# Gate logits from fp32 products of four column groups in place of products of high and low parts

## The chip, the cores and the metric

The kernel runs on one core of one Trainium2 chip. The metric is the device time of one execution in microseconds, as the median of several runs.

## The reference, cut to what matters

Three stages follow each other: a block-sparse attention, a dense first network, and a mixture of eight experts of which each token visits one, up to a capacity.

```python
def reference(**kwargs):
    ...
    x = np.ascontiguousarray(attn_out.transpose(0, 2, 1, 3)).reshape(B * S, H * D)   # 1088 tokens, 512 wide
    x = _moe_ref(x=x, **moe_kwargs)
    return _moe2_ref(x=x, **moe2_kwargs)

def _moe_ref(x, w1, w2, w3, w_out):
    h = np.maximum(np.maximum(x @ w1, x @ w2), x @ w3)      # 768 wide
    return (h @ w_out).astype(np.float32)                   # x2, 512 wide

def _moe2_ref(x, w_gate, w1, w2, capacity):
    logits = x @ w_gate                                     # 512 x 8
    expert_idx = np.argmax(logits, axis=1)
    ...                                                     # softmax weight of the chosen expert,
    for i in range(N):                                      # tokens to their expert, up to capacity
        ...
    h = np.maximum(np.einsum('ecd,edf->ecf', disp, w1), 0.0)
    y = np.einsum('ecf,efd->ecd', h, w2)
    ...
    for i in range(N):
        if keep[i]:
            out[i] = gate_w[i] * y[expert_idx[i], pos[i]]
    return out.astype(np.float32)
```

The change touches `logits = x @ w_gate`, one number per token and expert. An expert is chosen by argmax, so the logits have to keep nearly full fp32 accuracy.

## The kernel before

**Stages.** Up to about 118 us the attention runs on TensorE (PE), and between its parts, from 29 us on, the first layer of the dense network (`h`, L426); behind the first layer come its second layer, `x2` (L708), and the experts. Most products are made of three products of a faster type (fp32r): each fp32 number is split in a high part, rounded to fp32r, and a low part, the rest; high by high, high by low and low by high are summed in PSUM. ScalarE (ACT) usually makes the high part by a copy with a cast, VectorE (DVE) or GpSimd (POOL) the low part by a subtraction. Splits that the next stage waits for are those of `w_out` (`wo_h`, `wo_l`; the chain of L309 to L328 runs over ACT, DVE and POOL) and of the experts' weights (`w1h`, `w1l`, `w2h`, `w2l`; L828 and L829).

**The second layer.** `moe_second` walks over four windows of tokens: 256, 288, 256 and 288 columns (windows 0 to 3). In each it makes x2, transposed, in four blocks d of 128 of the 512 features; a block is 18 matmuls (L708) into one PSUM bank. ACT copies a finished block to `x2T[:, d]` in fp32 (L714), DVE makes its high and low part (`x2h`, `x2l`, both named `x2hl`, L715 and L716), and two matmuls (L699, called a pair here) add the block's share to the logits `pl`, one PSUM bank of 16 useful rows: the stationary side is `wgs[:, d]`, 128 columns of which 8 hold the high part of the gate's weights and the next 8 the low part, and the moving side is x2h, then x2l. `gate_weights` (L638 to L640) makes `wgs` on DVE at a place inside the first layer that a count sets.

**The tail of a window.** `tail_logits` makes the last pair (d = 3) and copies the 16 rows of `pl` to `lt`. After eight steps one matmul for each block of 128 (or 32) tokens (L738) turns `lt` by the constant `dup8`, 16 by 8, which also adds the high and the low rows, into `ptl`, and DVE copies it to `L` (L740). `tail_rows` transposes x2T back to rows of tokens (L748) and stores them.

**What sets the order.** Each engine runs its instructions in the order in which they are written. The code is a set of generators: a main one yields after each matmul, and `drive` lets side generators run after so many steps of it, so that their matmuls stand between those of the main one. The tail of window 0 runs in the second layer of window 1, that of window 1 in the last block of the first layer for windows 2 and 3, that of window 2 in the second layer of window 3. The tail of window 3 runs inside the first job of the experts: its last pair stands right behind the second layer (L1089), and `final` does the rest, the transposes of x2 (`px`), the second routing on DVE (`columns` L486 to L491, `rows_1` L496, `route`, `values`) and the placing of the tokens, between the matmuls of expert 0. The counts Y0 to Y4 are the steps that `final` waits between its parts.

**Expert 0.** Its tokens are gathered from DRAM by POOL, transposed by PE (`xp`, L803), cast by ACT (L805) and split by DVE (L806). Its first product is `ph` (L866): eight blocks f0 to f7 of 12 matmuls with 288 columns, whose ReLU and split `hhl` run on ACT and DVE and free the bank. All loads of weights go over the SP queue.

Of the kernel before, what the change touches and what calls it, by code (L numbers as in the profile page):

```python
# [7 lines left out]
F32 = mybir.dt.float32  # L8
F32R = mybir.dt.float32r
# [5 lines left out]
ALU = mybir.AluOpType  # L15
# [4 lines left out]
P = 128  # L20
# [6 lines left out]
NE = 8  # L27
# [19 lines left out]
def tile_block(ctx: ExitStack, tc: tile.TileContext, qk, qg, v, vo, vg, w123, w_out, w_gate, w1, w2, consts, out):  # L47
    nc = tc.nc
# [3 lines left out]
    const = ctx.enter_context(tc.tile_pool(name="const", bufs=1))  # L52
# [57 lines left out]
    cst = const.tile([P, NCONST - P - CM], F32, name="cst")  # L110
# [1 line left out]
    load_qg(0)  # L112
    dma_v(0)
    ident = cst[:, 0:P]
    dup8 = cst[0:16, 256:264]
    rev = cst[:, 264:272]
    valid = cst[:, 272:282]
    eidx = cst[:, 292:300]
# [4 lines left out]
    zero = mr.tile([P, P], F32, name="zero")  # L123
# [10 lines left out]
    iota_b = const.tile([P, P], BF16, name="iota_b")  # L134
    lowtri_b = const.tile([P, P], BF16, name="lowtri_b")
    ones_b = const.tile([P, P], BF16, name="ones_b")
    nc.gpsimd.memset(ones_b, 1.0)

    def routing_start():
# [354 lines left out]
    def rows_1(A, pm, nb):  # L494

        nc.vector.tensor_tensor(A, iota_b.unsqueeze(1).to_broadcast([P, nb, P]), pm.unsqueeze(2).to_broadcast([P, nb, P]), op=ALU.is_equal)  # L496
# [118 lines left out]
    k = 0  # L615
# [7 lines left out]
    s2 = phl.enter_context(tc.tile_pool(name="s2", bufs=1))  # L623
    ps_x = ctx.enter_context(tc.tile_pool(name="ps_x", bufs=2, space=PSUM))
    ps_y = ctx.enter_context(tc.tile_pool(name="ps_y", bufs=2, space=PSUM))
# [4 lines left out]
    hT[1] = (s2.tile([P, NF - NF1, NT], F32R, name="hTh1"), s2.tile([P, NF - NF1, NT], F32R, name="hTl1"))  # L630
    W["o"] = (s2.tile([P, NF, DM], F32R, name="wo_h"), s2.tile([P, NF, DM], F32R, name="wo_l"))

    wg = s2.tile([P, 4, NE], F32, name="wg")
    nc.sync.dma_start(wg, w_gate.rearrange("(c p) e -> p c e", p=P))
    wgs = s2.tile([P, 4, P], F32R, name="wgs")

    def gate_weights():
        nc.vector.tensor_copy(wgs, zero.unsqueeze(1).to_broadcast([P, 4, P]))  # L638
        nc.vector.tensor_copy(wgs[:, :, 0:NE], wg)
        nc.vector.tensor_tensor(wgs[:, :, NE : 2 * NE], wg, wgs[:, :, 0:NE].bitcast(F32), op=ALU.subtract)  # L640

    WIN2 = [(0, 256), (256, 288), (544, 256), (800, 288)]
    k = 0
    for f in range(NF1, NF):
        for c0, n in WIN2[: 2 if f == NF - 1 else 4]:
            for _ in moe_first(f, c0, n):
                tick()
                k += 1
                if k % 5 == 0:
                    take(ws, 1)  # L650
                if k == 100:
                    gate_weights()
    LATE = 0
    flush()
    while take(ws, 1):
# [5 lines left out]
    def x2_buf(wi):  # L661

        if wi < 2:
            return (
                s2b.tile([P, 4, 288], F32, tag="x2T", name=f"x2T{wi}"),
                [s2b.tile([P, 288], F32R, tag="x2hl", bufs=4, name=f"x2hl{wi}{i}") for i in range(4)],
                s2b.tile([16, 288], F32, tag="lt", name=f"lt{wi}"),
                [s2b.tile([P, 512], F32, tag="xs", bufs=6, name=f"xs{wi}{i}") for i in range(3)],
            )
        a = 288 * 4 * (wi - 2)  # L670
        return (
            rawb[:, a : a + 288 * 4].rearrange("p (d c) -> p d c", d=4),
            x2hl,
            rawb[0:16, 288 * (8 + wi - 2) : 288 * (9 + wi - 2)],
            [rawb[:, 288 * 12 + 512 * i : 288 * 12 + 512 * (i + 1)] for i in range(3)],
        )

    XB = {}
# [10 lines left out]
    def moe_second(c0, T):  # L689

        wi = [w[0] for w in WIN2].index(c0)
        XB[wi] = x2_buf(wi)
        x2T = XB[wi][0]
        pl_ = ps_y.tile([P, 512], F32, tag="py", name=f"pl{c0}")
        x2 = {}

        def logits(d):
            for k, x_ in enumerate(x2[d]):
                nc.tensor.matmul(pl_[:, :T], lhsT=wgs[:, d], rhs=x_[:, :T], start=d == 0 and k == 0, stop=d == 3 and k == 1)  # L699

        for d in range(4):
            po = ps_mm.tile([P, 512], F32, tag="mm", name=f"x2{c0}{d}")
            k = 0
            for f in range(NF):
                hh, hl = hT[f // NF1]
                f_ = f % NF1
                for w_, h_ in ((W["o"][0], hh), (W["o"][0], hl), (W["o"][1], hh)):
                    nc.tensor.matmul(po[:, :T], lhsT=w_[:, f, d * P : (d + 1) * P], rhs=h_[:, f_, c0 : c0 + T], start=k == 0, stop=k == 17)  # L708
                    k += 1
                    if k < 18:  # L710
                        yield
            x2h, x2l = XB[wi][1][2 * (d % 2) : 2 * (d % 2) + 2]
            x2[d] = (x2h, x2l)
            nc.scalar.copy(x2T[:, d, :T], po[:, :T])  # L714
            nc.vector.tensor_copy(x2h[:, :T], x2T[:, d, :T])  # L715
            nc.vector.tensor_tensor(x2l[:, :T], x2T[:, d, :T], x2h[:, :T].bitcast(F32), op=ALU.subtract)  # L716
            if d:
                logits(d - 1)
            yield
        TAIL.append((c0, T, x2T, pl_, logits))  # L720

    TAIL = []

# [3 lines left out]

    def tail_logits(wi):

        c0, T, x2T, pl_, logits = TAIL[wi]  # L730
        lt = XB[wi][2]
        if wi < 3:
            logits(3)
            nc.vector.tensor_copy(lt[:, :T], pl_[0:16, :T])
        yield 8
        ptl = ps_y.tile([P, 4, NE], F32, tag="py", name=f"ptl{c0}")
        for i, (c, n, row, blk) in enumerate(rows_of(wi)):
            nc.tensor.matmul(ptl[0:n, i], lhsT=lt[:, c - c0 : c - c0 + n], rhs=dup8, start=True, stop=True)  # L738
        for i, (c, n, row, blk) in enumerate(rows_of(wi)):
            nc.vector.tensor_copy(L[0:n, blk], ptl[0:n, i])  # L740

    def tail_rows(wi):

        c0, T, x2T, pl_, logits = TAIL[wi]
        for i, (c, n, row, blk) in enumerate(rows_of(wi)):
            pt = ps_x.tile([P, 4, P], F32, tag="px", name=f"px{c}")
            for d in range(4):
                nc.tensor.transpose(pt[0:n, d], x2T[:, d, c - c0 : c - c0 + n], ident)  # L748
            xs = XB[wi][3][i]
            nc.scalar.copy(xs[0:n], pt[0:n].rearrange("p d c -> p (d c)"))  # L750
            nc.sync.dma_start(x2d[row : row + n], xs[0:n])
            if row < S:
                nc.sync.dma_start(x2e[row : row + n], xs[0:n])
            yield 12
# [290 lines left out]
    IDS = [ids0] + [idsall[:, 3 * j : 3 * j + 3] for j in range(NE)]  # L1045
    rawb = pA.tile([P, NR * F2], F32, name="rawb")
    raw2 = [rawb[:, i * F2 : (i + 1) * F2] for i in range(NR)]
    x2hl = [pA.tile([P, 288], F32R, name=f"x2hl{i}") for i in range(4)]
    xg = [pA.tile([P if t < 2 else 32, DM], F32, name=f"xg{t}") for t in range(3)]
    xT = [pA.tile([P, 2, 4, CAP], F32R, name="xT0"), None]  # L1050
    wset(pA, 0)
# [34 lines left out]
            loads(96, (0, 5), (0, 6), (0, 7)), tokens0((126, 133, 194)),  # L1086
        ],
    )
    TAIL[3][4](3)  # L1089
    nc.vector.tensor_copy(XB[3][2], TAIL[3][3][0:16, :288])  # L1090
    rw.close()
    phl.close()

# [2 lines left out]
    xT[1] = pB.tile([P, 2, 4, CAP], F32R, name="xT1")  # L1096
    order = rt.tile([P, 2, NE], I32, name="order")

    Y0, Y1, Y2, Y3, Y4 = 10, 12, 44, 12, 3

    def final():

        hs_ = [pB.tile([P, 512], F32, tag="hs", bufs=2, name=f"sc{i}") for i in range(2)]
        As = [t.bitcast(BF16)[:, 256:896].rearrange("p (b m) -> p b m", b=5) for t in hs_]
        rows_1(As[0], columns(0, 5), 5)
        yield from tail_logits(3)
        c_ = yield from route(5, 10, ps_mm, "mm", 24)
        k_ = rt.tile([P, NE], F32, tag="key", name="key1")
# [69 lines left out]
def layout(inp):  # L1178
# [46 lines left out]
    masks = np.stack([np.where((blk == 6) | near & ok, 0.0, -8.0e9) for ok in (rel >= 0, True, rel < P)], axis=1)  # L1225
    tri = (np.arange(P)[None, :] > r).astype(float)
    dup = np.zeros((P, NE))
    dup[np.arange(16), np.arange(16) % 8] = 1.0
    valid = np.ones((P, 10))
    valid[32:, 0] = 0.0  # L1230
    valid[32:, 5] = 0.0
# [29 lines left out]
```

## Time and profile before

| | |
|---|---|
| median of 3 runs | 345.73 us (345.7 to 345.88) |
| the profiled execution | 347.64 us |
| its span in the trace | 345.9 us |
| granted clock of TensorE, mean | 0.98 |
| PE busy | 325.7 us (94%) |
| DVE busy | 251.0 us (73%) |
| ACT busy | 185.1 us (54%) |
| POOL busy | 141.5 us (41%) |

In the stages that the change touches, the profile divides like this (stretches of the trace, in us of its span, busy time of each engine, and the share of the DMA engines):

| stretch | what runs on PE | PE | DVE | ACT | DMA |
|---|---|---|---|---|---|
| 120 to 183 | first layer | 63.00 | 53.04 | 22.63 | 0.25 |
| 183 to 206 | second layer, windows 0 and 1 | 22.80 | 6.51 | 4.82 | 0.13 |
| 206 to 218 | last block of the first layer | 12.00 | 8.40 | 3.12 | 0.29 |
| 218 to 240 | second layer, windows 2 and 3 | 21.70 | 15.99 | 11.05 | 0.72 |
| 240 to 262 | expert 0, first product, second routing | 21.90 | 19.83 | 7.88 | 0.63 |
| 262 to 298 | experts 0 to 2 | 36.00 | 23.61 | 24.03 | 0.86 |

How to read it: a span is the time between the first and the last event of the trace, and the profiled execution is a little longer. The records of PE's matmuls overlap: one is shown 0.28 us long although the next starts 0.12 us behind it. So the cost of a matmul is the step from its start to the start of the next one, not its own length. A matmul in fp32 leaves two records, one in fp32r one. In a row, "128*32 128x64" is 128 rows by 32 columns of the stationary side, and 128 partitions by 64 columns of the moving one. The bracket at the end of a row is the time in which the engine stood idle before it, and who released it.

### The profile page before, as it was taken

Reading aid. Unit: us, or ns where it says so; the run is one execution under the profiler, and the core shown is the slowest. Engines: PE = TensorE matmul, PEld = TensorE weight load, DVE = VectorE, ACT = ScalarE, POOL = GpSimd, SP = SyncE. Lnnn points to the kernel's source line nnn. Section 1 sums busy time; section 2 is a strip of 40 time slices with the busy share of each in tenths; the row PEclk is TensorE's granted clock in tenths of the full one; section 3 lists DMA queues with packets and bytes.
Section 4 is the critical chain, followed back from the end, with each engine's and each line's share of the span. In section 5 each row is a group of like instructions: output and inputs, shape, how many; then the busy total and the mean of one; then the engine's idle time right before and its main releaser. Section 6 shows DMA issues by size and latency. Waiting matters only on the chain. (4 is left out here: it accounts for less than half of the span.)

```text
span 345.9 us, 8542 instructions
## 1 busy us (share of the span) xinstructions
PE 325.7 (94%) x3119; PEld 271.1 (78%) x3119; DVE 251.0 (73%) x662; ACT 185.1 (54%) x461; POOL 141.5 (41%) x168
## 2 busy tenths in 40 slices
PE   7989779999998999999999999999999999999990
PEld 2444547777787899999999999998987778777780
DVE  1777979985879448998993327867997893387881
ACT  3975666866675232423441223355525892488890
POOL 0375678664557517757784000310005542111211
PEclk9998987999999999999999999999999999999998
DMA  7975669490427913133300033665397999187100
GB/s 244 411 258 205 218 227 329 167 336 12 148 110 210 185 55 123 67 117 123 122 2 0 2 121 137 215 214 193 127 395 261 341 323 341 62 293 252 53 30 15
DMA packets 26293, 60.91 MB, mean 176 GB/s; under 512 B 3019, under 2 KB 8139, under 8 KB 26240
## 3 DMA queue, kind: packets, MB, share of 16 engines
q1 hardware_dynamic: 24640, 55.69, 46.8%
q0 software_dynamic: 1600, 4.54, 4.1%
q8 instruction: 30, 0.49, 0.6%
q14 instruction: 23, 0.19, 0.2%
HBM read 61.64 MB, written 7.47 MB: 200 GB/s over the span
## 5 line engine op out<-in xcount | busy, mean ns | idle before, releaser
L426 PE MATMUL h<-xh,wh 128*128 128x256 f32 (+1 forms) x288 | 84.6, 294 | 0.4 <-DVE hA L413 0.4
L426 PE MATMUL h<-xl,wh 128*128 128x256 f32 (+1 forms) x288 | 84.7, 294 | 0.0
L426 PE MATMUL h<-xh,wl 128*128 128x256 f32 (+1 forms) x288 | 84.3, 293 | 0.0
L426 PEld LDWEIGHTS h<-xl,wh 128*128 128x128 f32 x288 | 55.1, 191 | 0.9 <-issue 0.7
L426 PEld LDWEIGHTS h<-xh,wh 128*128 128x128 f32 x288 | 54.9, 191 | 1.1 <-DVE hA L413 0.6
L426 PEld LDWEIGHTS h<-xh,wl 128*128 128x128 f32 x288 | 55.0, 191 | 0.3 <-issue 0.2
L416 POOL TENSOR_TENSOR hTl<-hA,hTh 128x256 fp32r<-128x256 f32 (+1 forms) x24 | 19.3, 802 | 58.0 <-ACT hTh L415 57.1
L791 POOL DMA_INDIRECT xg<-x2d,idsall x12 | 14.6, 1220 | 60.8 <-DMA rawb<-in_w_dram 33.3
L829 DVE TENSOR_TENSOR w1l<-rawb,w1h 128x1024 fp32r<-128x1024 f32 x20 | 24.0, 1226 | 11.6 <-ACT w1h L828 11.6
L921 PE MATMUL py<-w2h,hhl 128*128 128x512 f32 x112 | 29.7, 395 | 0.0
L415 ACT CAST hTh<-hA 128x256 fp32r<-128x256 f32 (+1 forms) x24 | 10.0, 418 | 35.2 <-DVE hA L413 35.2
L829 DVE TENSOR_TENSOR w2l<-rawb,w2h 128x1024 fp32r<-128x1024 f32 x23 | 27.4, 1218 | 1.9 <-ACT w2h L828 1.8
L226 POOL CAST xh<-xs 128x128 fp32r<-128x128 f32 x32 | 13.1, 409 | 37.7 <-ACT xs L224 37.7
L708 PE MATMUL x<-hTl,wo_h 128*128 128x256 f32 (+1 forms) x96 | 28.2, 294 | 0.0
L708 PE MATMUL x<-hTh,wo_l 128*128 128x256 f32 (+1 forms) x96 | 27.9, 291 | 0.2 <-POOL wo_l L328 0.2
L708 PE MATMUL x<-hTh,wo_h 128*128 128x256 f32 (+1 forms) x96 | 27.8, 290 | 0.0
L188 ACT ACTIVATE sm<-sm,nm 128x128 f32<-128x128 f32 x64 | 25.2, 399 | 4.7 <-DVE nm L183 4.6
L327 POOL TENSOR_TENSOR ct<-ct,wh 128x512 f32<-128x512 f32 x18 | 25.6, 1420 | 1.5 <-DVE ca L324 1.5
L413 DVE TENSOR_TENSOR hA<-hA,h 128x256 f32<-128x256 f32 (+1 forms) x48 | 20.7, 431 | 7.2 <-PE h L426 6.5
L328 POOL TENSOR_TENSOR wl<-ct,ca 128x512 fp32r<-128x512 f32 x18 | 23.9, 1329 | 2.9 <-DVE ca L326 1.6
L921 PEld LDWEIGHTS py<-w2h,hhl 128*128 128x128 f32 x112 | 20.9, 188 | 4.5
L183 DVE CUSTOM_DVE_ANT_0 sm<-s,mask 128x128 f32<-128x128 f32 x64 | 15.9, 285 | 10.4 <-PE s L171 10.0
(213 smaller groups left out, 767.3 us busy)
## 6 DMA issues: line engine op xcount, KB each, us to landing
rawb<-in_w_dram SPq DMA_DIRECT2D x51, 512.0 KB
raww<-in_w_dram SPq DMA_DIRECT2D x18, 512.0 KB
rawv<-in_v_dram SPq DMA_DIRECT2D x16, 512.0 KB
qk<-in_qk_dram SPq DMA_DIRECT2D x16, 320.0 KB
rawo<-in_w_out_dram SPq DMA_DIRECT2D x6, 512.0 KB
rw<-in_w_dram SPq DMA_DIRECT2D x5, 512.0 KB
out_dram<-zero SPq DMA_DIRECT2D x1, 2176.0 KB
rawg<-in_vo_dram SPq DMA_DIRECT2D x4, 512.0 KB
```

What stands on the lines that cost most here:

```text
L183: nc.vector.tensor_tensor_reduce(sm[:, j], ps[:, j, 0:P], mk, scale=-0.125, scalar=3.0e38, op0=ALU.add, op1=ALU.min, accum_out=nm[:, j : j ...
L188: nc.scalar.activation(sm[:, j], sm[:, j], AF.Exp, bias=nm[:, j : j + 1], scale=-1.0, accum_out=ssum[:, j : j + 1])
L226: nc.gpsimd.tensor_copy(dst[0], xs)
L327: nc.gpsimd.tensor_tensor(tf, tf, hi.bitcast(F32), op=ALU.subtract)
L328: nc.gpsimd.tensor_tensor(lo, tf, b.bitcast(F32), op=ALU.add)
L413: nc.vector.tensor_tensor(hA[:, :T], hA[:, :T], ph[:, :T], op=ALU.max)
L416: nc.gpsimd.tensor_tensor(hl[:, f_, c0 : c0 + T], hA[:, :T], dst.bitcast(F32), op=ALU.subtract)
L426: nc.tensor.matmul(ph[:, :T], lhsT=w_[:, a], rhs=x_[:, c, c0 : c0 + T], start=n == 0, stop=n == 11)
L708: nc.tensor.matmul(po[:, :T], lhsT=w_[:, f, d * P : (d + 1) * P], rhs=h_[:, f_, c0 : c0 + T], start=k == 0, stop=k == 17)
L791: nc.gpsimd.indirect_dma_start(out=xg[t], out_offset=None, in_=src, in_offset=bass.IndirectOffsetOnAxis(ap=IDS[j][0:n, t, 0:1].bitcast(I32 ...
L829: nc.vector.tensor_tensor(l_, raw_of(j, k), h_.bitcast(F32), op=ALU.subtract)
L921: nc.tensor.matmul(py[0:nt], lhsT=a[:, c, a0 : a0 + nt], rhs=w_[:, c], start=i == 0, stop=i == 23)
```

## The change

`wg` moves to a tile of 128 x 4 x 32 fp32 that is set to zero at the start (by POOL) and takes the gate's weights in the first 8 of each 32 columns. `gate_weights`, `wgs`, the split of x2 and the pairs inside `moe_second` go. `tail_logits` now makes all logits of a window: four fp32 matmuls, d = 0 to 3, each with the 32 columns `wg[:, d]` and the whole window of `x2T[:, d]`, write to the partitions 32 d to 32 d + 31 of one bank, `pl`. DVE copies all 128 rows to `lt`, and the matmuls that turn `lt` take 128 rows and a `dup8` of 128 by 8, which adds the four groups. The pair at L1089 and its copy at L1090 go; for window 3 the set of four stands in `final` behind a new `yield 4`, and Y2 falls from 44 to 40.

```diff
-    dup8 = cst[0:16, 256:264]
+    dup8 = cst[:, 256:264]
...
+    wg = const.tile([P, 4, 32], F32, name="wg")
+    nc.gpsimd.memset(wg, 0.0)
...
-    wg = s2.tile([P, 4, NE], F32, name="wg")
-    nc.sync.dma_start(wg, w_gate.rearrange("(c p) e -> p c e", p=P))
-    wgs = s2.tile([P, 4, P], F32R, name="wgs")
-
-    def gate_weights():
-        nc.vector.tensor_copy(wgs, zero.unsqueeze(1).to_broadcast([P, 4, P]))
-        nc.vector.tensor_copy(wgs[:, :, 0:NE], wg)
-        nc.vector.tensor_tensor(wgs[:, :, NE : 2 * NE], wg, wgs[:, :, 0:NE].bitcast(F32), op=ALU.subtract)
+    nc.sync.dma_start(wg[:, :, 0:NE], w_gate.rearrange("(c p) e -> p c e", p=P))
...
-                if k == 100:
-                    gate_weights()
...
     def moe_second(c0, T):
...
-        pl_ = ps_y.tile([P, 512], F32, tag="py", name=f"pl{c0}")
-        x2 = {}
-
-        def logits(d):
-            for k, x_ in enumerate(x2[d]):
-                nc.tensor.matmul(pl_[:, :T], lhsT=wgs[:, d], rhs=x_[:, :T], start=d == 0 and k == 0, stop=d == 3 and k == 1)
-
         for d in range(4):
...
-            x2h, x2l = XB[wi][1][2 * (d % 2) : 2 * (d % 2) + 2]
-            x2[d] = (x2h, x2l)
             nc.scalar.copy(x2T[:, d, :T], po[:, :T])
-            nc.vector.tensor_copy(x2h[:, :T], x2T[:, d, :T])
-            nc.vector.tensor_tensor(x2l[:, :T], x2T[:, d, :T], x2h[:, :T].bitcast(F32), op=ALU.subtract)
-            if d:
-                logits(d - 1)
             yield
...
     def tail_logits(wi):
 
-        c0, T, x2T, pl_, logits = TAIL[wi]
-        lt = XB[wi][2]
-        if wi < 3:
-            logits(3)
-            nc.vector.tensor_copy(lt[:, :T], pl_[0:16, :T])
+        c0, T, x2T = TAIL[wi]
+        lt = XB[wi][1]
+        pl_ = ps_y.tile([P, 512], F32, tag="py", name=f"pl{c0}")
+        for d in range(4):
+            nc.tensor.matmul(pl_[32 * d : 32 * d + 32, :T], lhsT=wg[:, d], rhs=x2T[:, d, :T], start=True, stop=True)
+        nc.vector.tensor_copy(lt[:, :T], pl_[:, :T])
         yield 8
...
-    TAIL[3][4](3)
-    nc.vector.tensor_copy(XB[3][2], TAIL[3][3][0:16, :288])
...
-    Y0, Y1, Y2, Y3, Y4 = 10, 12, 44, 12, 3
+    Y0, Y1, Y2, Y3, Y4 = 10, 12, 40, 12, 3
 
     def final():
...
         rows_1(As[0], columns(0, 5), 5)
+        yield 4
         yield from tail_logits(3)
         c_ = yield from route(5, 10, ps_mm, "mm", 24)
...
-    dup[np.arange(16), np.arange(16) % 8] = 1.0
+    dup[np.arange(P), np.arange(P) % 32 % NE] = np.arange(P) % 32 < NE
```

On PE, in window 0: its last pair and the matmuls of its tail stand in the second layer of window 1. Before:

```order
L708 MATMUL x_3221<-hTl_2507,wo_h 128x288
L699 MATMUL pl_3116<-x2hl_3110,wgs 128x256
L699 MATMUL pl_3116<-x2hl_3111,wgs 128x256
L708 MATMUL x_3221<-hTh_2506,wo_l 128x288
L708 MATMUL x_3221<-hTh_2506,wo_h 128x288
L708 MATMUL x_3221<-hTl_2507,wo_h 128x288
L708 MATMUL x_3221<-hTh_2506,wo_l 128x288
L708 MATMUL x_3246<-hTh_141,wo_h 128x288
L708 MATMUL x_3246<-hTl_142,wo_h 128x288
L708 MATMUL x_3246<-hTh_141,wo_l 128x288
L708 MATMUL x_3246<-hTh_141,wo_h 128x288
L738 MATMUL ptl_3251<-cst,lt_3112 128x8 x2
```

And now:

```order
L692 MATMUL x_3194<-hTl_2509,wo_h 128x288
L712 MATMUL pl_3209<-x2T_3104,wg 32x256 x4
L692 MATMUL x_3194<-hTh_2508,wo_l 128x288
L692 MATMUL x_3194<-hTh_2508,wo_h 128x288
L692 MATMUL x_3194<-hTl_2509,wo_h 128x288
L692 MATMUL x_3194<-hTh_2508,wo_l 128x288
L692 MATMUL x_3220<-hTh_143,wo_h 128x288
L692 MATMUL x_3220<-hTl_144,wo_h 128x288
L692 MATMUL x_3220<-hTh_143,wo_l 128x288
L692 MATMUL x_3220<-hTh_143,wo_h 128x288
L717 MATMUL ptl_3225<-cst,lt_3105 128x8 x2
```

At the place of the pair of d = 3 now stands one set of four, and the three pairs ahead of it (not in these rows) are gone; the two matmuls that turn lt stay where they were.

On PE, from the last product of x2 in window 3 into expert 0's first product (x is the last product, xp the transpose of expert 0's last 32 tokens, px the transposes of x2 to rows). Before:

```order
L708 MATMUL x_3800<-hTh_2506,wo_l 128x288
L699 MATMUL pl_3698<-x2hl_3519,wgs 128x288
L699 MATMUL pl_3698<-x2hl_3520,wgs 128x288
L803 MATMUL xp_3838<-cst,xg_3525 128x32 x4
L699 MATMUL pl_3698<-x2hl_3521,wgs 128x288
L699 MATMUL pl_3698<-x2hl_3522,wgs 128x288
L866 MATMUL ph<-xT_3526,w1h_3527 128x288 x4
L866 MATMUL ph<-xT_3526,w1l_3528 128x288 x3
L748 MATMUL px_3883<-cst,rawb 32x128 x4
L866 MATMUL ph<-xT_3526,w1l_3528 128x288
L866 MATMUL ph<-xT_3526,w1h_3527 128x288
L738 MATMUL ptl_3892<-cst,rawb 32x8
```

And now:

```order
L692 MATMUL x_3738<-hTh_2508,wo_l 128x288
L782 MATMUL xp_3772<-cst,xg_3486 128x32 x4
L845 MATMUL ph<-xT_3487,w1h_3488 128x288 x4
L845 MATMUL ph<-xT_3487,w1l_3489 128x288
L712 MATMUL pl_3812<-rawb,wg 32x288 x4
L845 MATMUL ph<-xT_3487,w1l_3489 128x288 x2
L727 MATMUL px_3820<-cst,rawb 32x128 x4
L845 MATMUL ph<-xT_3487,w1l_3489 128x288
L845 MATMUL ph<-xT_3487,w1h_3488 128x288 x5
L717 MATMUL ptl_3837<-cst,rawb 32x8
L717 MATMUL ptl_3837<-cst,rawb 128x8 x2
```

The two pairs ahead of ph are gone, the set of four stands five matmuls into ph, px keeps its place behind seven matmuls of ph, and ptl stands four of them later.

On DVE, from the split of expert 0's last tokens into the second routing (L486 to L496 are its columns and rows, w2l the split of weights of expert 0). Before:

```order
L715 CAST x2hl_3521<-rawb 128x288
L716 TENSOR_TENSOR x2hl_3522<-rawb,x2hl_3521 128x288
L806 TENSOR_TENSOR xT_3526<-xp_3838,xT_3526 128x4x32
L1090 COPY rawb<-pl_3698 16x288
L486 TENSOR_SCALAR pct<-pos_all 128x5
L487 SCALAR_TENSOR_TENSOR pct<-pos_all,pct 128x5
L488 SCALAR_TENSOR_TENSOR pcm<-pct,pos_all 128x5
L490 TENSOR_SCALAR col_all<-pos_all 128x5
L491 TENSOR_TENSOR col_all<-col_all,pct 128x5
L496 TENSOR_TENSOR sc_3864<-iota_b,pcm 128x640
L829 TENSOR_TENSOR w2l_3530<-rawb,w2h_3529 128x1024
L740 COPY L<-ptl_3892 32x8
```

And now:

```order
L785 TENSOR_TENSOR xT_3487<-xp_3772,xT_3487 128x4x32
L488 TENSOR_SCALAR pct<-pos_all 128x5
L489 SCALAR_TENSOR_TENSOR pct<-pos_all,pct 128x5
L490 SCALAR_TENSOR_TENSOR pcm<-pct,pos_all 128x5
L492 TENSOR_SCALAR col_all<-pos_all 128x5
L493 TENSOR_TENSOR col_all<-col_all,pct 128x5
L498 TENSOR_TENSOR sc_3795<-iota_b,pcm 128x640
L808 TENSOR_TENSOR w2l_3491<-rawb,w2h_3490 128x1024
L713 COPY rawb<-pl_3812 128x288
L850 SCALAR_TENSOR_TENSOR hhl<-ph,hhl 128x256
L852 SCALAR_TENSOR_TENSOR hhl<-ph,hhl 128x32
L719 COPY L<-ptl_3837 32x8
```

The split of x2 is gone, the columns and rows of the routing come first, and the copy of pl (128 rows for 16) comes behind the split of w2, next to the first block of expert 0's hhl.

## Rows read from the trace of the kernel before

**Rows 1.** Waits of PE, 183 to 346 us: line waited for: total us, times, longest us

```profile
PE acc L887 <- PEq L988: 0.6, 2, 0.3
...
PE pl L699 <- DVE x2hl L715: 0.2, 1, 0.2
PE x L708 <- POOL wo_l L328: 0.2, 1, 0.2
```

**Rows 2.** Windows: us, PE, PEld, DVE, ACT, POOL busy (count), clock, DMA, GB/s

```profile
264.00:280.00 16.00, 16.00 (x79) 11.91 (x78) 14.76 (x16) 13.78 (x19) 7.13 (x6) 1.00 0.97 351
```

**Rows 3.** Chain of waits: start us, us, step

```profile
187.07 0.24 PE pl L699 x2
...
197.14 0.44 PE px L748 x4
...
198.23 0.26 PE pl L699 x2
```

**Rows 4.** Timeline of PE at 109 us: start us, us, instruction; then line 277's durations

```profile
109.64 0.30 PE L426 MATMUL h<-xh,wl 128*128 128x288 f32 x1
109.86 0.65 PE L277 MATMUL gpv<-rawg,gph 128*32 128x64 f32 x32
110.45 0.31 PE L277 MATMUL gpv<-rawgg,gph 32*32 32x64 f32 x8
110.69 0.40 PE L426 MATMUL h<-xh,wh 128*128 128x288 f32 x1
110.93 0.29 PE L426 MATMUL h<-xl,wh 128*128 128x288 f32 x1
...
L277 PE MATMUL gpv<-rawg,gph x128: 219/219/243, 70.0 to 118.3; 128*32 128x64 f32 x128
```

**Rows 5.** Timeline of PE, windows 0 and 1: the matmuls that turn lt

```profile
194.93 0.29 PE L708 MATMUL x<-hTh,wo_h 128*128 128x288 f32 x1
195.15 0.61 PE L738 MATMUL ptl<-cst,lt 16*128 16x8 f32 x4
...
195.92 0.30 PE L708 MATMUL x<-hTh,wo_l 128*128 128x288 f32 x1
...
207.02 0.76 PE L738 MATMUL ptl<-cst,lt 16*128 16x8 f32 x6
```

**Rows 6.** Timeline of DVE at 151 us; then its longest wait, 150 to 184 us

```profile
151.31 0.45 DVE L638 CAST wgs<-zero 128x512 fp32r<-128x512 f32 x1
...
153.10 0.41 DVE L413 TENSOR_TENSOR hA<-hA,h 128x256 f32<-128x256 f32 x1
...
DVE cap L311 <- ACT cap L309: 1.5, 4, 0.5
```

**Rows 7.** Timeline of PE at 184 us: the second layer's first window

```profile
184.05 0.28 PE L708 MATMUL x<-hTl,wo_h 128*128 128x256 f32 x1
184.53 0.39 PE L708 MATMUL x<-hTh,wo_l 128*128 128x256 f32 x1 [0.20 <-POOL wo_l L328]
```

**Rows 8.** Waits of DVE, 239 to 262 us, the longest

```profile
DVE x2hl L715 <- ACT rawb L714: 0.5, 1, 0.5
```

**Rows 9.** Timeline of all engines behind the last product of x2

```profile
238.07 0.29 PE L708 MATMUL x<-hTh,wo_l 128*128 128x288 f32 x1
...
238.40 0.40 ACT L714 COPY rawb<-x 128x288 f32<-128x288 f32 x1 [0.75 <-PE x L708]
...
238.55 0.43 PE L803 MATMUL xp<-cst,xg 32*128 32x32 f32 x4
...
239.02 0.27 ACT L805 CAST xT<-xp 128x128 fp32r<-128x128 f32 x1 [0.22 <-PE xp L803]
...
239.93 0.69 PE L866 MATMUL ph<-xT,w1h 128*128 128x288 f32 x4
```

**Rows 10.** Timeline of DVE, the second routing's start

```profile
240.50 0.15 DVE L486 TENSOR_SCALAR pct<-pos_all 128x5 f32<-128x5 f32 x1
...
243.12 0.29 DVE L740 COPY L<-ptl 32x8 f32<-32x8 f32 x3
```

More of the change, by code (lines that the diff above doesn't have):

```diff
@@ L665, in x2_buf @@
                 s2b.tile([P, 4, 288], F32, tag="x2T", name=f"x2T{wi}"),
-                [s2b.tile([P, 288], F32R, tag="x2hl", bufs=4, name=f"x2hl{wi}{i}") for i in range(4)],
-                s2b.tile([16, 288], F32, tag="lt", name=f"lt{wi}"),
+                s2b.tile([P, 288], F32, tag="lt", name=f"lt{wi}"),
                 [s2b.tile([P, 512], F32, tag="xs", bufs=6, name=f"xs{wi}{i}") for i in range(3)],
@@ L672, in x2_buf @@
             rawb[:, a : a + 288 * 4].rearrange("p (d c) -> p d c", d=4),
-            x2hl,
-            rawb[0:16, 288 * (8 + wi - 2) : 288 * (9 + wi - 2)],
+            rawb[:, 288 * (8 + wi - 2) : 288 * (9 + wi - 2)],
             [rawb[:, 288 * 12 + 512 * i : 288 * 12 + 512 * (i + 1)] for i in range(3)],
@@ L711, in moe_second @@
                         yield
-            x2h, x2l = XB[wi][1][2 * (d % 2) : 2 * (d % 2) + 2]
-            x2[d] = (x2h, x2l)
             nc.scalar.copy(x2T[:, d, :T], po[:, :T])
-            nc.vector.tensor_copy(x2h[:, :T], x2T[:, d, :T])
-            nc.vector.tensor_tensor(x2l[:, :T], x2T[:, d, :T], x2h[:, :T].bitcast(F32), op=ALU.subtract)
-            if d:
-                logits(d - 1)
             yield
-        TAIL.append((c0, T, x2T, pl_, logits))
+        TAIL.append((c0, T, x2T))
     TAIL = []
@@ L742, in tail_rows @@
     def tail_rows(wi):
-        c0, T, x2T, pl_, logits = TAIL[wi]
+        c0, T, x2T = TAIL[wi]
         for i, (c, n, row, blk) in enumerate(rows_of(wi)):
@@ L748, in tail_rows @@
                 nc.tensor.transpose(pt[0:n, d], x2T[:, d, c - c0 : c - c0 + n], ident)
-            xs = XB[wi][3][i]
+            xs = XB[wi][2][i]
             nc.scalar.copy(xs[0:n], pt[0:n].rearrange("p d c -> p (d c)"))
@@ L1047, in tile_block @@
     raw2 = [rawb[:, i * F2 : (i + 1) * F2] for i in range(NR)]
-    x2hl = [pA.tile([P, 288], F32R, name=f"x2hl{i}") for i in range(4)]
     xg = [pA.tile([P if t < 2 else 32, DM], F32, name=f"xg{t}") for t in range(3)]
```

## The prediction

> **What bounds the kernel now.** I read the waits of TensorE (PE) from 183 us to the end first. Of 162 us it waited 1.4 us in all: 0.2 us for the last low part of w_out and 0.2 us for a part of x2, which this change can reach, and 1.0 us at two branches late in the program, of which the rows show the larger [rows 1]. No row there names a DMA. So from 183 us on the time is what PE's own instructions take, and an instruction taken off it comes off the end, unless something else then becomes late. Second, the stretch from 264 to 280 us: the DMA engines are 97% busy, but PE is busy for all 16.00 us [rows 2]; DMA is close to the limit there and not over it. Third, VectorE (DVE): from 239 to 262 us its longest wait was 0.5 us, for ScalarE's copy of x2 [rows 8]; it runs almost back to back through the second routing, and PE gains nothing by getting ahead of it.
>
> **Old products.** A window's logits take eight matmuls, two for each 128 columns of x2. The chain of waits has a pair at 0.24 us in a window of 256 columns and at 0.26 us in one of 288 [rows 3], of which some pairs take 0.27. All four pairs make 0.94 us (windows 0 and 2, where two of four are 0.23) and 1.06 us (window 1). In window 3 two pairs, 0.54 us, stand ahead of the last product of x2 (start 238.07 us, called T below); the other two come behind it and are counted there.
>
> **New products.** Four fp32 matmuls of 128 rows and 32 columns each, one per column group. The kernel has this form already, with 64 moving columns, in the attention's global queries [rows 4]. There 16 matmuls leave 32 records, two to a matmul, and lie in one row of 0.65 us; one record takes 0.22 us, so the 32 starts spread over 0.43 us. One after another, at the 0.86 ns a column of the fp32 transposes (0.44 us for four of 128 columns [rows 3]), 32 records of 64 columns would need 1.8 us. They go four at a time: eight rounds, 0.055 us a round. A set for 256 columns is two rounds of four times that, 0.44 us, and for 288 columns 0.50 us. Around it: the step from the product ahead to the first of the group is 0.22 us where 0.13 is usual (0.09 more); from the group's start to the next form 0.59 us, which is the 0.43, a last round of 0.055 and 0.10 of emptying; the product behind takes 0.24 us to its next instead of 0.13 (0.11 more); 0.02 for the four starts [rows 4]. Together 0.76 us (256) and 0.82 us (288). Net: -0.18 us in windows 0 and 2, -0.24 in window 1.
>
> The row thus shows four column groups at full concurrency. The Trainium skill's page "TensorE: Matmul & The Clock Gate", section "Measured speedup vs the span model", gives three column tiles only 2.38 times the speed of one; by that a round would be some 1.3 times as long (an estimate from that page). No run here has four column groups with more than 64 moving columns on 128 rows.
>
> **Transposing the logits.** The small matmuls that turn lt (two blocks, four records) now have 16 rows and switch the array's form: from 194.93 to 195.92 us, 0.99 us less two steps of 0.13, is 0.73 us [rows 5]. With 128 rows they have the form of the products around them; four records of 128 columns are then like the four transposes of a block, 0.44 us [rows 3]. That is -0.29 us in windows 0 and 2. Windows 1 and 3 have a third block of 32 columns, 0.15 us more now (0.76 against 0.61) [rows 5]; that matmul keeps a form of its own (128 by 32), so entry and exit stay. I take -0.10 us there; bounds 0 and -0.35.
>
> **The split of the gate's weights goes.** Its three DVE instructions run from 151.31 to 153.10 us, 1.79 us [rows 6]. DVE was behind from there to 182 us: its longest wait is 1.5 us for ScalarE, in four pieces [rows 6], and that ScalarE work itself follows DVE. At the end of this chain PE waits for wo_l: 184.05 to 184.53 us, 0.36 us over a step, and 0.10 us after it [rows 7]. With DVE 1.8 us ahead I take all 0.46 us as gone; bounds 0 and -0.46.
>
> **Up to T.** 0.46 (wo_l) + 0.47 (window 0: 0.18 + 0.29) + 0.34 (window 1) + 0.47 (window 2) + 0.54 (window 3) = 2.28 us. The sixteen pairs of DVE instructions that split x2 also go. I price them at nothing up to T: PE's one wait for them is 0.2 us long and lies behind T, in the third pair of window 3 [rows 1].
>
> **From T on.** Now the first product of expert 0 (ph) starts at 239.93, T + 1.86: it stands behind the last four logit products, which wait for the split of x2 [rows 9]. After the change, only the transpose of the last 32 tokens (0.48 us behind T now, 0.22 without the pair between; 0.43 long) and ScalarE's cast of it stand ahead. The cast begins when the copy of x2 ends, near T + 0.73, takes 0.27 us (239.02 before) [rows 9], and ph starts near T + 1.06: 0.80 us gained. Then PE does the window's set, 0.82, inside expert 0's first product. DVE now begins its columns at 240.50, T + 2.43, and reaches the copies of L at 243.12 [rows 10]; after the change it can begin near T + 1.30. The 2.62 us of work there now come before the copy of the logits, which so starts near T + 3.9 and ends at T + 4.35; PE reaches the small matmuls at T + 4.05 and waits 0.3 us, a new wait. DVE waits some 0.2 us for the ReLU of expert 0 and 0.3 us for these matmuls, so the 1.1 us that it began earlier go: 0.45 for the copy, 0.5 in those waits. It reaches the fourth block of expert 0, which frees the bank that PE needs, at the same distance from T as before. So behind T the gain is 0 (bounds +0.4 and -0.3): PE's 0.8 us are eaten by the set and by DVE.
>
> **Later.** From 264 us on the loads of weights are issued as splits free their buffers; those splits follow PE, so all move by the same 2.3 us. The fill of wg on GpSimd and the larger copy cost nothing: the first is at the start, the copy has the same 256 or 288 columns on each partition.
>
> **Sum.** 2.28 us, say 2.3. The profiled execution took 347.64 us (span 345.9); its sum is 345.3 us (span 343.6). The runs shown have a median of 345.73, 1.9 us below it, since a profiled execution takes longer; the same difference gives **343.4 us**.
>
> **Rivals.**
> - *Slowed groups.* The four groups read four streams of 1 KB per partition at once and hold each other up with long streams. With rounds 1.3 times as long, a set costs 0.13 to 0.15 us more, three of them 0.4 us: 343.8 us. This is what the skill's page gives. Against it: rounds of 64 columns show nothing of the kind [rows 4]. Chance 9%.
> - *DVE's second routing is late.* The copy of the logits stands behind a split of w2; if ScalarE's cast for it is late, or the ReLU makes DVE wait longer, DVE loses the 1.1 us of its earlier start once more, and PE waits at the seventh or eighth block of expert 0. Then 343.4 + 1.1 = 344.5 us. For it: DVE has no slack there [rows 8]. Chance 11%.
> - *DMA takes the gain.* If the loads from 264 to 280 us (97% busy) cannot be had earlier, PE waits for expert 2's weights and gives back nearly all: 345.5 us. Against it: no wait for DMA there now. Chance 10%.
> - *The groups run one after another* (slower). A fp32 matmul is two records; should both of a group end before the next group begins, a set has eight rounds for two. 256 columns take 0.22 us a round: 8 x 0.22 = 1.76 for 0.44, +1.32 us; 288: +1.49. Up to T +4.1 us, and in window 3 PE is then later than DVE by about 1.5: 345.73 - 2.3 + 5.6 = 349.0 us. From rounds about 2.2 times as long (1.88 us of rounds up to T, 2.28 us of gain to lose) the change costs time; here it is 4. Against it stand the 32 records in 0.65 us. Chance 6%.
>
> **Chances.** The forecast itself 64%, with its own bounds 342.6 to 344.2 (wo_l not gained, 32-column matmul dearer; or the 0.3 us behind T gained and the small matmuls cheaper). Faster by over 0.2%, which is 0.7 us and about what a measurement tells from no change: forecast, slowed groups and late routing, 0.83 with a little left for mishaps; within 0.2%: 0.10; slower: 0.07. The range is 342.5 to 345.0: it holds the forecast and the first two rivals, and leaves out about 2 in 10.
>
> **What would show it.** Right: the set of four in a window leaves eight records whose starts lie within 0.3 us, and the next product of x2 starts 0.7 to 0.85 us after the one ahead of the set would have ended; no wait of PE for wo_l at 184 us; ph starts about 1.1 us after the last product of x2; the small matmuls take 0.45 us. Wrong: starts of the eight records spread over more than 1 us; a wait of PE for DVE of over 0.5 us between ph and the second product of expert 0; a wait for a DMA behind 264 us.

## The result, and the profile after

The changed kernel took 343.59 us (median of 12 runs, 342.8 to 346.1), the one before 346.1 us beside it (12 runs, 345.61 to 348.2). The ratio is 0.9915 with an interval of 0.9892 to 0.9937: between 2.2 and 3.7 us faster. Forecast were 343.4 us and a gain of 2.3.

The profiled execution of after took 342.99 us (span 341.1). The two traces can be laid over each other from the first product of x2 on, and from there to the last matmul each place repeats within 0.1 us from one profile of a kernel to the next. This table gives the time since that product (a matmul's start, read from the timelines of PE):

| | before | after | difference |
|---|---|---|---|
| first product of x2, in the span | 182.15 | 179.69 | |
| first product of window 1 | 9.78 | 8.62 | -1.16 |
| T, the last product of x2 | 55.92 | 53.62 | -2.30 |
| first ph, expert 0's first product | 57.78 | 54.63 | -3.15 |
| first py, expert 0's second product | 73.45 | 70.85 | -2.60 |
| last matmul | 155.12 | 152.55 | -2.57 |

The timeline of PE of after, at window 0's set and at the matmuls that turn it (the columns are those of [rows 4]; the first row is the start of the second layer):

```profile
179.69 0.28 PE L692 MATMUL x<-hTh,wo_h 128*128 128x256 f32 x1
...
190.03 0.29 PE L692 MATMUL x<-hTl,wo_h 128*128 128x288 f32 x1
190.25 0.64 PE L712 MATMUL pl<-x2T,wg 128*32 128x256 f32 x8
190.82 0.40 PE L692 MATMUL x<-hTh,wo_l 128*128 128x288 f32 x1
191.06 0.30 PE L692 MATMUL x<-hTh,wo_h 128*128 128x288 f32 x1
...
191.85 0.29 PE L692 MATMUL x<-hTh,wo_h 128*128 128x288 f32 x1
191.98 0.51 PE L717 MATMUL ptl<-cst,lt 128*128 128x8 f32 x4
192.34 0.38 PE L692 MATMUL x<-hTl,wo_h 128*128 128x288 f32 x1
192.56 0.30 PE L692 MATMUL x<-hTh,wo_l 128*128 128x288 f32 x1
```

From 190.03 to 191.06 us are 1.03 us; two steps of 0.13 off, the set costs 0.77 us. The turn (the small matmuls that turn lt), from 191.85 to 192.56, costs 0.45 after the same subtraction, against 0.73 in [rows 5].

The waits of PE in after, from 183 us to the end, all that the view lists; shorter ones, of up to 0.15 us, show only as a longer step from one matmul to the next:

```profile
PE acc L866 <- PEq L967: 0.6, 2, 0.3
PE acc L866 <- PEq L969: 0.4, 1, 0.4
PE ph L845 <- ACT xT L784: 0.4, 1, 0.4
```

Both waits of [rows 1] that hung on the split are gone; a wait for the cast of expert 0's last tokens has come. No DMA is among them, although its engines are as full as in [rows 2]. The same stretch of after, which now lies 5 us earlier:

```profile
259.00:275.00 16.00, 16.00 (x80) 11.91 (x79) 14.75 (x16) 13.76 (x19) 6.69 (x6) 1.00 0.98 343
```

Behind T, all engines of after, to compare with [rows 9, 10]; the last two rows are the split of expert 0's fourth block on DVE and the first py:

```profile
233.32 0.29 PE L692 MATMUL x<-hTh,wo_l 128*128 128x288 f32 x1
233.54 0.43 PE L782 MATMUL xp<-cst,xg 32*128 32x32 f32 x4
233.64 0.40 ACT L696 COPY rawb<-x 128x288 f32<-128x288 f32 x1 [0.74 <-PE x L692]
234.00 0.27 ACT L784 CAST xT<-xp 128x128 fp32r<-128x128 f32 x1
234.32 0.79 PE L845 MATMUL ph<-xT,w1h 128*128 128x288 f32 x4 [0.35 <-ACT xT L784]
234.51 0.16 DVE L488 TENSOR_SCALAR pct<-pos_all 128x5 f32<-128x5 f32 x1
235.18 0.69 PE L712 MATMUL pl<-rawb,wg 128*32 128x288 f32 x8
237.14 0.45 DVE L713 COPY rawb<-pl 128x288 f32<-128x288 f32 x1
237.65 0.77 PE L717 MATMUL ptl<-cst,rawb 128*32 128x8 f32 x6
237.97 0.42 DVE L850 SCALAR_TENSOR_TENSOR hhl<-ph,hhl 128x256 fp32r<-128x256 f32 x1 [0.38 <-ACT hhl L849]
...
248.22 0.42 DVE L850 SCALAR_TENSOR_TENSOR hhl<-ph,hhl 128x256 fp32r<-128x256 f32 x1
...
250.55 0.62 PE L900 MATMUL py<-w2h,hhl 128*128 128x512 f32 x2
```

ph starts at T + 1.00 where it started at T + 1.86. Of these 0.86 us little is left at py: T + 17.23, against T + 17.53 before.

### The profile page after: what moved, and what is told of

It reads as the page before. It is cut to its first block, busy times and chain, and to the rows that moved or that the text cites. A ratio compares the mean times of both kernels' runs of the same rounds, so it can differ in the third digit from the quotient of the medians.

```text
span 341.1 us, 8500 instructions
## 1 busy us (share of the span) xinstructions
PE 319.7 (94%) x3119; PEld 265.6 (78%) x3119; DVE 238.4 (70%) x627; ACT 184.9 (54%) x461; POOL 141.8 (42%) x169
## 4 chain that ended last, share of the span: by engine, by line
PE 61%; DMA 18%; DVE 9%; issue 6%; ACT 2%; POOL 1%; SPq 0%; POOLq 0%; ACTq 0%
PE h L428 29%; PE x L692 11%; DMA xg<-x2d,idsall 8%; DMA out_dram<-y,idsall 8%; PE ph L845 3%; PE s L173 3%; PE sgp L242 3%; PE pv L215 2%; PE pt L201 2%; PE py L900 2%; DVE ca L313 2%; PE pxq L223 1%; DMA qg<-in_qg_dram 1%; DVE ct L319 1%; PE px L727 1%
## 5 line engine op out<-in xcount | busy, mean ns | idle before, releaser
L807 ACT CAST w2h<-rawb 128x1024 fp32r<-128x1024 f32 x23 | 23.4, 1048 | 0.0
```

What stands on the lines that cost most here:

```text
L807: nc.scalar.copy(h_, raw_of(j, k))
```

## The experiments

All differences below are read from the profiles, counted from the first product of x2, where they repeat; the times of single executions differ by some 3 us, for a reason that the first experiment shows in large part.

**Is the attention shorter?** The first product of x2 stands 2.46 us earlier in after, which the change cannot explain by an instruction. The kernel before was profiled once more.

> The kernel before, profiled once more. Its first trace shows the first product of x2 (the second layer's first matmul) at 182.15 us, the trace of after shows it at 179.69, 2.46 us earlier, although the change touches next to nothing ahead of it. Theory: these 2.46 us are the clock, which was granted at 0.66 from 25 to 30 us and at 0.83 from 40 to 60 us in the first trace of before and at 1.00 in after; a profile of before without such a stretch has its first product of x2 near 179.7 us, and from there to the last matmul 155.1 us as in the first trace. Rival: the change itself makes the attention 2.5 us shorter; then the first product of x2 stands near 182.2 us at a clock of 1.00 too.

The second profile lost still more clock, so the expected 179.7 us did not come. The stretch from 20 to 65 us (the columns are those of [rows 2]; the clock is the third number from the end) in after, in before with the small matmuls on 128 rows (an experiment below), in before, and in before again:

```profile
20.00:65.00 45.00, 36.41 (x601) 23.82 (x601) 41.19 (x140) 31.57 (x119) 32.96 (x44) 1.00 0.68 233
```

```profile
20.00:65.00 45.00, 37.74 (x598) 24.54 (x587) 40.92 (x140) 31.50 (x119) 33.39 (x44) 0.96 0.70 235
```

```profile
20.00:65.00 45.00, 38.69 (x575) 23.84 (x578) 38.87 (x136) 30.91 (x115) 31.21 (x43) 0.89 0.64 221
```

```profile
20.00:65.00 45.00, 39.25 (x565) 23.90 (x553) 38.11 (x136) 30.54 (x114) 30.84 (x42) 0.85 0.63 221
```

The first product of x2 stands at 179.69, 179.84, 182.15 and 183.17 us in these four: the lower the clock, the later. PE's own work takes longer there: 38.69 us busy for 575 instructions in before, 36.41 us for 601 in after. The second kernel is one of before's own kind and stands where after stands, while the other kernels built on after stand at 180.3 to 183.7. So most of this place goes with the clock that is granted in the attention, and nothing points to the change. The clock does not explain all of it: two kernels at 1.00 stand at 179.69 and 180.28, and four at 0.96 between 179.84 and 181.35. Up to 1.5 us stay without a cause. From the first product of x2 on the second profile of before gives 155.12 us to the last matmul, the very number of the first.

**The split of the gate's weights and wo_l.** Two kernels, from both sides. In after, the three instructions come back at their old place, read by nothing:

```diff
+    def gate_weights():
+        nc.vector.tensor_copy(wgs, zero.unsqueeze(1).to_broadcast([P, 4, P]))
+        nc.vector.tensor_copy(wgs[:, :, 0:NE], wg[:, :, 0:NE])
+        nc.vector.tensor_tensor(wgs[:, :, NE : 2 * NE], ...)
...
+                if k == 100:
+                    gate_weights()
```

> After, with the three DVE instructions that split the gate's weights put back at their old place (their output is read by nothing). Theory: DVE is late again and PE waits again for wo_l in the first window, 0.36 us and 0.10 us behind it: from the first product of x2 to the first product of window 1 it takes 9.07 us (after 8.62, before 9.78), and all that follows is later by 0.45 us. Rival: the wait for wo_l hung on the 32 splits of x2 or on the place of the logits, not on the split of the gate's weights; then 8.62 us stay.

Window 1 begins 9.03 us behind the first product (after 8.62), 0.41 us later, the last matmul is 0.51 us later, and the wait is back:

```profile
182.97 0.28 PE L701 MATMUL x<-hTl,wo_h 128*128 128x256 f32 x1
183.41 0.39 PE L701 MATMUL x<-hTh,wo_l 128*128 128x256 f32 x1 [0.16 <-POOL wo_l L330]
```

In before, the same instructions move behind the last split of w_out:

```diff
-                if k == 100:
-                    gate_weights()
...
     while take(ws, 1):
         pass
+    gate_weights()
```

> Before, with the split of the gate's weights moved from inside the first layer to its end, behind the split of w_out, all else as in before. Theory: the wait of PE for wo_l goes by the move alone: from the first product of x2 to the first of window 1 it takes 9.78 - 0.46 = 9.32 us, and the rest follows 0.46 us earlier. Rival: the wait hangs on something else: 9.78 us.

9.32 us, the number expected, no wait of PE from 175 to 200 us, and the last matmul 0.44 us earlier. So 0.41 (put back) to 0.45 us (moved) of the change's gain hang on the place of 1.8 us of DVE work, far from the logits, and could have been had without the change.

**The turn alone.** Before with 128 rows in the copy and in the small matmuls:

```diff
-    dup8 = cst[0:16, 256:264]
+    dup8 = cst[:, 256:264]
...
-            nc.vector.tensor_copy(lt[:, :T], pl_[0:16, :T])
+            nc.vector.tensor_copy(lt[:, :T], pl_[:, :T])
```

> Before, with one part of the change alone: all 128 rows of the logits' bank are copied and the small matmuls that turn them take 128 rows. Theory: each turn of two blocks gets 0.29 us cheaper and that with a third block 0.19 (after shows this): from the first product of x2 to T 55.92 - 0.77 = 55.15 us; behind T the 0.2 us of the last turn are lost since PE follows DVE there, so to the first matmul of expert 0's second product 73.45 - 0.77 = 72.7 us. Rival: the copy of 128 rows in place of 16 costs DVE what PE wins; then 73.4.

T came 0.80 us earlier (55.12; 0.06 of it lie in window 0, ahead of any turn, where nothing was changed), py 0.79 (72.66), the last matmul 0.79. The turn in this kernel:

```profile
192.56 0.29 PE L708 MATMUL x<-hTh,wo_h 128*128 128x288 f32 x1
192.69 0.51 PE L738 MATMUL ptl<-cst,lt 128*128 128x8 f32 x4
193.06 0.38 PE L708 MATMUL x<-hTl,wo_h 128*128 128x288 f32 x1
193.27 0.29 PE L708 MATMUL x<-hTh,wo_l 128*128 128x288 f32 x1
```

The copy of eight times as many rows takes DVE 0.01 us more (0.425 for 0.411 with 256 columns). A third of what the change gains up to T is the form of these small matmuls, and not the logits' products.

**Without the column groups.** After, with the fp32 products on 128 columns, 120 of them zero:

```diff
-    wg = const.tile([P, 4, 32], F32, name="wg")
+    wg = const.tile([P, 4, P], F32, name="wg")
...
-            nc.tensor.matmul(pl_[32 * d : 32 * d + 32, :T], ..., start=True, stop=True)
+            nc.tensor.matmul(pl_[:, :T], ..., start=d == 0, stop=d == 3)
```

> After, with the same four fp32 products a window on 128 columns of the stationary side (8 useful, the rest zero), summed in one bank in place of four column groups at once. Theory: a set is then eight records one after another, 0.22 us each for 256 columns and 0.25 for 288, so 1.76 and 1.98 us in place of 0.76 and 0.82: from the first product of x2 to T 53.63 + 1.0 + 1.16 + 1.0 = 56.8 us (before 55.92), and about 1.1 us more behind T: 345.73 - 2.3 + 4.3 = 347.7 us in time, slower than before. Rival: fp32 by itself is cheap here and the groups don't matter; then T stays within 0.5 us of 53.6 and the time near 343.6.

The time was 347.79 us (10 runs) against 347.19 of before beside it (13 runs), ratio 1.0034, interval 1.0012 to 1.0057: slower than before. That the time expected was met to 0.1 us is luck: 2.0 us above before were expected, and the medians are 0.6 apart, the last matmuls 1.5, while before itself ran 1.5 us longer here than the 345.73 of the forecast. The products themselves are sure: T stands at 56.63, 3.01 us later than in after and 0.71 later than in before, and the last matmul at 156.66. Window 0's set:

```profile
190.79 0.29 PE L692 MATMUL x<-hTl,wo_h 128*128 128x288 f32 x1
190.92 1.89 PE L712 MATMUL pl<-x2T,wg 128*128 128x256 f32 x8
192.46 0.48 PE L692 MATMUL x<-hTh,wo_l 128*128 128x288 f32 x1
192.78 0.29 PE L692 MATMUL x<-hTh,wo_h 128*128 128x288 f32 x1
```

From 190.79 to 192.78 us, two steps off, it costs 1.73 us, one record after the other, where the groups take 0.77. Without them the fp32 products lose; with them they win. This is also the price that the rival of groups one after another had put on a set (1.76 us).

**The split of x2.** After with the 32 instructions of DVE put back, read by nothing:

```diff
             nc.scalar.copy(x2T[:, d, :T], po[:, :T])
+            x2h, x2l = ...
+            nc.vector.tensor_copy(x2h[:, :T], x2T[:, d, :T])
+            nc.vector.tensor_tensor(x2l[:, :T], x2T[:, d, :T], x2h[:, :T].bitcast(F32), op=ALU.subtract)
```

> After, with the 16 pairs of DVE instructions that split x2 put back (about 12 us of DVE, read by nothing; in the last two windows two buffers in place of four). Theory: up to the last product of x2 (T) nothing changes, 53.63 us from the first product of x2 to T; behind T DVE begins the second routing some 0.75 us later, and since PE there follows DVE (the bank that the fourth block's split frees), the first matmul of expert 0's second product comes 0.6 to 0.8 us later: 71.5 us from the first product of x2 (after 70.86). Rival: behind T the time is PE's own; then 70.9 us.

T stays (53.58). py comes at 71.28, 0.43 us later. That the time follows DVE is right; the size and the place of the wait were not. DVE begins the columns of the second routing 0.49 us later, counted from T, not 0.75, since in after it waits for the cast of expert 0's tokens where it now splits:

```profile
235.47 0.31 DVE L699 CAST x2hl<-rawb 128x288 fp32r<-128x288 f32 x1 [0.45 <-ACT rawb L697]
...
236.40 0.16 DVE L488 TENSOR_SCALAR pct<-pos_all 128x5 f32<-128x5 f32 x1
```

And PE does not lose this time at the bank that the fourth block's split frees, but earlier, where it waits for DVE's copy of the logits ahead of the turn:

```profile
239.53 0.77 PE L721 MATMUL ptl<-cst,rawb 128*32 128x8 f32 x6 [0.56 <-DVE rawb L717]
```

The turn begins 0.44 us later than in after, and py comes as far behind it as there (12.89 us; 12.90 in after).

**Getting the 0.86 us behind T.** Two moves in after, each alone and then both. First, the transposes of expert 0's last tokens stand ahead of the last four products of x2:

```diff
-            ... tokens0((126, 133, 194)),
+            ... tokens0((126, 133, 139)),
```

> After, with the transposes of expert 0's last 32 tokens five products of x2 ahead of T in place of behind it, so that their cast is done when PE gets to expert 0. Theory: PE's wait for this cast (0.35 us and 0.10 of restart) goes, and DVE, on which PE hangs behind T, begins its routing some 0.5 us earlier: from the first product of x2 to the first matmul of expert 0's second product 70.86 - 0.45 = 70.4 us, 0.1 per cent in time. Rival: DVE, now waiting longer for expert 0's first ReLU, gives nothing back, and PE waits as long at a later place: 70.8 us.

py at 70.38, 0.47 us earlier than in the first profile of after and 0.40 than in the second (70.78, below), and the wait for the cast is gone. In time 343.17 us (6 runs), 0.9911 of before (0.9881 to 0.994), which cannot be told from after's 0.9915.

Second, window 3's set four products of expert 0 earlier:

```diff
-    Y0, Y1, Y2, Y3, Y4 = 10, 12, 40, 12, 3
+    Y0, Y1, Y2, Y3, Y4 = 10, 12, 44, 12, 3
...
         rows_1(As[0], columns(0, 5), 5)
-        yield 4
         yield from tail_logits(3)
```

> After without the four steps of waiting ahead of window 3's set (Y2 back at 44): the set stands behind the first product of expert 0 in place of the fifth. Theory: DVE copies the logits ahead of the split of w2 in place of behind it, so PE's wait of 0.15 us ahead of the turn goes, and DVE waits less for the first ReLU: to the first matmul of expert 0's second product 70.86 - 0.2 to 0.4 = 70.5 to 70.7 us. Rival: PE reaches the set too early and waits for the copy of x2: 70.9 us or more.

py at 70.59, 0.26 us earlier (0.19 than in the second profile of after). Both, with `yield 2` and Y2 = 42:

> After, with both moves: the transposes of expert 0's last 32 tokens five products of x2 earlier, as in the run before, and two steps of waiting ahead of window 3's set in place of four (Y2 42), so that DVE copies the logits ahead of the split of w2. Theory: the gains of 0.47 and 0.26 us, measured alone, add up as far as PE does not wait for the copy of x2, which ends 0.73 us behind T while PE gets to the set 0.6 us behind it: from the first product of x2 to the first matmul of expert 0's second product 70.85 - 0.6 = 70.2 us, bounds 70.1 and 70.4; in time some 0.5 to 0.6 us under after. Rival: behind T there is one floor, that of PE's own work, which the first move alone reached; then 70.4.

py at 70.55: 0.30 us earlier than in after and 0.17 later than with the first move alone, each from one profile. The gains do not add up. Whether the rival's floor is there stays open: PE's ordinary steps behind T were 133 ns long in this run, for 131 with the first move alone, which makes some 0.2 us over its 85 such steps. Beside that, DVE has a longer wait in it, for the matmuls that turn the logits:

```profile
241.78 0.30 DVE L719 COPY L<-ptl 32x8 f32<-32x8 f32 x3 [0.72 <-PE ptl L717]
```

where with the first move alone it lost 0.36 us to the ReLU. DVE begins this copy 0.26 us earlier than with the first move alone, but the split of expert 0's first block, which came ahead of it there, now comes behind it (10.18 us from the copy to the fourth block's split, for 9.76), so DVE reaches the fourth block 0.15 us later. In time 343.13 us (6 runs) beside 344.16 of after (8 runs) on the same chip; ratios to before 0.9898 (0.9858 to 0.9937) and 0.9908 (0.9878 to 0.9939), not apart. What was expected of after, run again there:

> After once more, on the same chip as the run with both moves. From the first product of x2 to the last matmul 152.55 us as in its first trace; the place of the first product of x2 follows the clock granted ahead of it: 179.7 us where none of it is lost, 1 to 3 us later where it is.

152.46 us to the last matmul, 0.09 less than in the first profile of after (py at 70.78); the first product of x2 at 180.88, with a granted clock as low as 0.54 in one stretch of five us ahead of it.

**Who sets py.** From the first product of x2, in us: the start of the fourth block's split on DVE, the first py, and the first matmul of the turn. The last column is how long PE's eight products across the start of expert 0's eighth block take, where PE needs the bank that this split frees:

| kernel | split of block four | first py | between | turn | turn to py | eight products |
|---|---|---|---|---|---|---|
| before | 71.13 | 73.45 | 2.32 | 59.49 | 13.96 | 1.55 |
| after | 68.52 | 70.85 | 2.33 | 57.95 | 12.90 | 1.29 |
| after, x2 split put back | 68.97 | 71.28 | 2.32 | 58.39 | 12.89 | 1.26 |
| after, tokens earlier | 68.06 | 70.38 | 2.32 | 57.49 | 12.89 | 1.27 |
| after, set earlier | 68.23 | 70.59 | 2.36 | 57.23 | 13.35 | 1.20 |
| after, both | 68.21 | 70.55 | 2.33 | 57.23 | 13.32 | 1.28 |
| after, gate split put back | 68.89 | 71.31 | 2.42 | 58.31 | 13.00 | 1.23 |

The eight products in before, in after and in after with the set earlier:

```profile
253.15 1.55 PE L866 MATMUL ph<-xT,w1h 128*128 128x288 f32 x8
```

```profile
248.35 1.29 PE L845 MATMUL ph<-xT,w1h 128*128 128x288 f32 x8
```

```profile
249.10 1.20 PE L845 MATMUL ph<-xT,w1h 128*128 128x288 f32 x8
```

The distance alone does not show who leads. With the set earlier the steps of PE from one product to the next are all 0.13 us there, so it waits for nothing: 1.20 us is the products' own time, and py follows PE's own work. With the split of the gate's weights put back (ordinary steps of 133 ns) it waits for nothing either, at a distance of 2.42 us. In before PE lost 0.35 us to the split of the fourth block; in after 0.09 is left. What remains of PE's waiting for DVE in after lies ahead of the turn: its step into the turn is 0.37 us, where 0.22 to 0.23 is usual, and 0.86 with the split of x2 put back. In these two and with the tokens earlier py follows the turn at 12.89 or 12.90 us. So in after DVE sets the time behind T at the turn: shown, with work added to DVE (the turn 0.44 us later, py 0.43) and with DVE begun earlier (0.46 and 0.47). From the turn on PE and DVE reach the eighth block within 0.1 us of each other, so behind the turn neither of them alone sets the time.

## Why the prediction was right, step by step

- **The old and the new products.** Right in size. A set measured 0.77 us for 256 columns and, in window 1 by the same subtraction, 0.82 for 288, as forecast (0.76 and 0.82) from rows of 64 columns [rows 4]. In after's row the eight records of a set last 0.64 us and one of them 0.38, so their starts lie within 0.26 us, under the 0.3 named as the sign. The rival of slowed groups falls: from the first record's start to the fifth's, which is one round of four and the small steps between the groups, the trace has 0.24 us for 256 columns, and one record alone takes 0.216 in the kernel without groups (1.73 / 8). The Trainium skill's page "TensorE: Matmul & The Clock Gate", section "Measured speedup vs the span model", has 2.38 times for three column tiles. A round here shows some 3.6 times for four (4 x 0.216 / 0.24), which differs; the whole set, with what it costs to enter and leave the form, shows 1.73 / 0.77 = 2.2, which is near it, though for four tiles. In the rival of groups one after another the 1.88 us of rounds hold the set of window 3, which lies behind T; up to T it is 1.38, so with this sum alone the change would cost time from rounds 2.7 times as long, not 2.2.
- **Turning the logits.** Right for two blocks: 0.73 to 0.45 us, -0.28 for -0.29. With a third block it was -0.19 and not -0.10 (window 1, from the product ahead of the turn to the second behind it: 1.13 us before, 0.94 after): taken too small, within its bounds.
- **The gate's weights.** 0.41 and 0.45 us for 0.46, right and shown from both sides.
- **Up to T.** 2.28 forecast, 2.30 measured (2.35 in the second profile of after). The gate's weights (0.45) and the turn (0.80, measured alone) leave 1.05 us for the products, where 1.14 were forecast.
- **From T on.** Right in that little of PE's gain is left at py, and in part in why. ph gained 0.86 for 0.80, and the set inside ph takes most of it (0.83). PE waited 0.15 us ahead of the turn for the forecast 0.3; DVE waited 0.38 us for the ReLU for the forecast 0.2, and not at all for the turn, for the forecast 0.3. DVE reached the fourth block not at the same distance from T but 0.31 us nearer (15.21 before, 14.90 after), and the 0.35 us that PE lost there fell to 0.09, so behind T there were 0.3 us to gain, not 0. That is the one term of the sum that was clearly off, and it lay within its bound of 0.4.
- **DMA and the late routing.** Neither rival came. No wait for DMA appeared from 183 us on, and DVE was early, not late.
- **The step from the profile to the time failed**, without hurting the sum. The forecast said that a profiled execution takes 1.9 us longer than the others. After's took 342.99 us, less than the median of its own runs. Before's profile had lost clock in the attention (0.89 from 20 to 65 us), and after's had not (1.00). The forecast for after's profile, 345.3 us, was therefore 2.3 too high, while the median that was wanted, where this difference was taken off again, came out right. From the first product of x2 to the last matmul the change is worth 2.57 us; the medians say 2.5, the ratio 2.9. That the time was met within 0.2 us is partly luck: before's median was 346.1 us and not the 345.73 that the forecast started from, and the gain was larger by 0.2 to 0.6, and the two nearly cancel.

## What to carry to other kernels

Small fp32 products that each need few columns cost less here as four column groups at once than as fp32r products of high and low parts (0.77 for 0.94 us), but only as groups: the same products on the full width made the kernel slower than before. Add up a change like this from its parts, because here some 0.45 us came from DVE instructions that were in the way of another chain and 0.8 from the row count of some tiny matmuls, and each could be had alone. Where two engines lean on each other, as PE and DVE do behind T, a constant distance between them does not tell who leads: follow PE's steps and look for each place where one is longer than usual, because a change can move the wait from one place to another, as here from the eighth block to the turn.

## What was not expected of the hardware

- With a granted clock of 0.5 to 0.9 of full speed in single stretches between 25 and 60 us the whole rest of the kernel stood up to 4 us later from profile to profile (first product of x2 at 179.69 to 183.74 us), while the places from there to the last matmul repeated within 0.1 us for the same kernel. Effects under 1 us could be read from a profile's later part, not from medians.
- The fp32 matmuls that turn the logits cost 0.45 us on 128 rows and 0.73 on 16 rows, though they read eight times as much. The forecast had this size and gave as its reason that they keep the form of the products around them. The experiment changes only the number of rows and shows the size; it does not show the reason.
